# A second MLP whose second products take seven block products for eight in half of its quads, with the order of work found by a list pass of the builder

## The chip, the cores and the metric

The kernel runs on one core of a Trainium2 chip. The time is that of one execution on the device in microseconds, the median of several runs of the same program. One execution was profiled as well; all rows below are of that one.

## The reference

Three stages follow one another, all in float32: an attention without softmax, gated by u, and two MLPs over the same 6016 tokens.

```python
# u, v: (2, 3008, 256); z: (2, 3008, 64); S = 3008
scores = (1.0 / S) * np.matmul(z, z.transpose(0, 2, 1))
x = u * np.matmul(np.maximum(scores, 0.0) ** 2, v)
x = x.reshape(6016, 256)
# first MLP: w_in (256, 2048), w_out (2048, 256), s, b: one number each
r = np.maximum(x @ w_in, 0.0)
x = (s * (r * r) + b) @ w_out
# second MLP: weights of its own of the same shapes
h = x @ w_in2
out = (h * (1.0 / (1.0 + np.exp(-1.702 * h)))) @ w_out2
```

## The kernel before

**Products.** Each float32 operand is split into a high and a low part of the reduced matmul type (fp32r): the high part is a copy by ScalarE (ACT), the low part a subtraction by VectorE (DVE). A block product of 128 by 128 by 512 is then three matmuls of TensorE (PE): low by high, high by low, high by high, all summed in one bank of PSUM. The weights come as float64 and are decoded first by a handful of bit operations (`decode_w`).

**Tiles and stages.** The tokens stand in 12 chunks of 512 (the last two 448), and the MLPs work on pairs of chunks. The hidden 2048 columns are 16 blocks of 128. A *quad* is two hidden blocks by the two chunks of a pair, so a pair has 8 quads. In program order come the attention, the first two chunks of the first MLP (`Mlp`), its other five pairs, and the six pairs of the second MLP: 11 pairs of quads. Layer 0 is the first MLP, layer 1 the second.

**A quad's first product** (`Quad.up`, matmuls in `product`, L672) is a two by two product of blocks and already takes seven block products in place of eight, by sums of weights (s1 to s4, `sum_w`) and of tokens (t1 to t4, `parts_of`); its seven products, 21 matmuls, go into the four banks ps_a to ps_d. ACT saves a bank to SBUF (`save`, L720), DVE adds a saved bank to another one (`join`, L730), ACT applies the activation (L744, L752), and the four values c11, c21, c12, c22 are split into high (L760, ACT) and low (L761, DVE). A bank must have been read before the next product can begin in it.

**A quad's second product** (`Quad.down`, `add_hidden`, L542) takes the four values by the blocks of w_out: eight block products, 24 matmuls, into accumulators accq (two sets of two banks), which sum over the eight quads of a pair. `post` stores the end result: y in layer 0 (L566), the transposed output in layer 1 (L580).

**What sets the order.** The engines each work in the order in which the program issues their instructions. The builder walks over steps (four for a quad), and the second product of a step runs 5 steps behind its first. What lies between is put at a numbered step with a rank in it (`later`, `due`), loads and the splitting of weights at numbers worked out by hand (`when`, `todo`). The split weights of the layer at work are held in SBUF (the 32 tiles of `ring`, the sums in four wide tiles); DMAs of the MLPs are issued by one queue on SyncE (SP).

Of the kernel before, what the change touches and what calls it, by code (L numbers as in the profile page):

```python
# [15 lines left out]
def attention_mlp_mlp_kernel(  # L16
# [24 lines left out]
    nc = tc.nc  # L41
# [16 lines left out]
    WARM = 16  # L58
    NQ = NF // 2
    NP = NM // 2  # L60
    assert DQ == 64 and TAIL == 64 and D == 2 * P and NKT == TPC * NCH
# [4 lines left out]
    mid = ctx.enter_context(tc.tile_pool(name="mid", bufs=1))  # L66
    bits = ctx.enter_context(tc.tile_pool(name="bits", bufs=1))
    ew = ctx.enter_context(tc.tile_pool(name="ew", bufs=2))
# [14 lines left out]
    def mid_tile(name, dtype=F32):  # L83
        kind = name[0]
        return mid.tile([P, CH], dtype, tag="w" if kind == "w" else "zu", name=name, bufs=5 if kind == "w" else 4)
# [24 lines left out]

    u_rows = u.rearrange("b s d -> (b s) d")
# [10 lines left out]
    def load_z(bb, t):  # L122
        n = width(t)
        z0 = begin(bb, t)
        zr = mid_tile(f"zr_{bb}_{t}").rearrange("p (t a) -> p t a", a=32)
# [15 lines left out]
    def split_z(bb, t, part):  # L141
        if part == 0:
            zr = staged.pop(("z", bb, t))
            zt = staged["zt", bb, t] = mid_tile(f"zt_{bb}_{t}")
# [47 lines left out]
    def load_u(m, h):  # L192
        start, n = tokens(m)
        ur = mid_tile(f"ur_{m}_{h}").rearrange("p (t a) -> p t a", a=32)
        for i in range(4):
            nc.sync.dma_start(
                out=ur[32 * i : 32 * i + 32, : n // 32, :],
                in_=u_rows[start : start + n, h * P + 32 * i : h * P + 32 * i + 32].rearrange(
                    "(t b) a -> b t a", b=32
                ),  # L200
            )
        staged["u", m, h] = ur

    def gate(m, h):
        n = tokens(m)[1]
        ur = staged.pop(("u", m, h))
        ut = mid_tile(f"ut_{m}_{h}")
        if m < 2 * LASTC:
            nc.vector.transpose(
                out=ut.rearrange("p (t g a) -> p t g a", t=4, g=4),  # L210
                in_=ur.rearrange("p (g t) a -> p t g a", g=4),
            )
        else:
            nc.vector.transpose(out=ut[:, :n], in_=ur[:, : n // 32, :].rearrange("p t a -> p (t a)"))
        x = xT[m][:, h, :n]
        nc.vector.tensor_tensor(out=x, in0=x, in1=ut[:, :n], op=ALU.mult)


# [3 lines left out]
    def load_w(layer, j, k):  # L222
        w = ((w_in1, w_out1), (w_in2, w_out2))[layer][k].bitcast(U32)
        raw = mid_tile(f"wr_{layer}_{j}_{k}", U32)
        if k == 0:
            src = w[:, j * 2 * P : (j + 1) * 2 * P].rearrange("(k p) f -> p k f", p=P)
            nc.sync.dma_start(out=raw.rearrange("p (k f) -> p k f", k=2), in_=src)
        else:
            nc.sync.dma_start(out=raw, in_=w[j * P : (j + 1) * P, :])
        staged["w", layer, j, k] = raw.rearrange("p (n w) -> p w n", w=2)  # L230

    def decode_w(layer, j, k, part):

        raw = staged["w", layer, j, k]
        low, high = raw[:, 0, :], raw[:, 1, :]
        if part == 0:
            pw = staged["pw", layer, j, k] = bits.tile([P, CH // 2], U32, tag="pw", name="pw")
            nc.vector.tensor_scalar(pw, high, 20, 0x7FF, ALU.logical_shift_right, ALU.bitwise_and)  # L240
        elif part == 1:
            pw = staged["pw", layer, j, k]
            nc.scalar.activation(out=pw, in_=pw, func=AF.Relu, scale=float(2**23), bias=rebias[:, 0:1])
            mt = staged["mt", layer, j, k] = bits.tile([P, CH // 2], U32, tag="mt", name="mt")
            nc.vector.tensor_scalar(mt, high, 0xFFFFF, 0x100000, ALU.bitwise_and, ALU.bitwise_or)
        elif part == 2:
            mt = staged["mt", layer, j, k]
            fr = staged["fr", layer, j, k] = bits.tile([P, CH // 2], F32, tag="fr", name="fr")
            nc.vector.scalar_tensor_tensor(fr, low, 2.0**-32, mt, ALU.mult, ALU.add)
        elif part == 3:  # L250
            pw = staged["pw", layer, j, k]
            nc.vector.scalar_tensor_tensor(pw, high, 0x80000000, pw, ALU.bitwise_and, ALU.bitwise_or)
        else:
            pw, fr = staged["pw", layer, j, k], staged["fr", layer, j, k]
            if k == 0:
                staged["wf", layer, j] = mid_tile(f"wf_{layer}_{j}")
            half = staged["wf", layer, j].rearrange("p (k n) -> p k n", k=2)[:, k, :]
            nc.vector.scalar_tensor_tensor(half, fr, 2.0**-20, pw.bitcast(F32), ALU.mult, ALU.mult)
            if k == 1:
                staged["done", layer, j] = staged.pop(("wf", layer, j))  # L260

    def store_w(layer, j):
        wf[layer, j] = hbm.tile([P, CH], F32, tag=f"wf_{layer}_{j}", name=f"wfh_{layer}_{j}")
        nc.sync.dma_start(out=wf[layer, j], in_=staged.pop(("done", layer, j)))

    def fetch_w(layer, j):
        staged["wf", layer, j] = mid_tile(f"wb_{layer}_{j}")
        nc.sync.dma_start(out=staged["wf", layer, j], in_=wf[layer, j])

    def sum_w(layer, i, part):  # L270

        if part:
# [742 lines left out]
```

## Time and profile before

| | |
|---|---|
| median of 3 runs | 1446.21 us (1444.78 to 1446.44) |
| profiled execution | 1447.46 us, of which its span 1445.7 us |
| TensorE busy | 1432.8 us (99%) |
| ScalarE busy | 1089.7 us (75%) |
| VectorE busy | 1062.3 us (73%) |
| mean of the granted TensorE clock | 0.999 of full speed |

The span runs from the first to the last instruction in the trace; the 1.76 us besides are outside it. A busy time counts an instant once, also where the modelled ends of matmuls overlap. The quads take the time from about 553 us to the end; before that come the attention and the first two chunks of the first MLP.

### The profile page before, as it was taken

Reading aid. Unit: us, or ns where it says so; the run is one execution under the profiler, and the core shown is the slowest. Engines: PE = TensorE matmul, PEld = TensorE weight load, DVE = VectorE, ACT = ScalarE, POOL = GpSimd, SP = SyncE. Lnnn points to the kernel's source line nnn. Section 1 sums busy time; section 2 is a strip of 40 time slices with the busy share of each in tenths; the row PEclk is TensorE's granted clock in tenths of the full one; section 3 lists DMA queues with packets and bytes.
Section 4 is the critical chain, followed back from the end, with each engine's and each line's share of the span. In section 5 each row is a group of like instructions: output and inputs, shape, how many; then the busy total and the mean of one; then the engine's idle time right before and its main releaser. Section 6 shows DMA issues by size and latency. Waiting matters only on the chain.

```text
span 1445.7 us, 19096 instructions
## 1 busy us (share of the span) xinstructions
PE 1432.8 (99%) x6404; PEld 1199.6 (83%) x6404; DVE 1062.3 (73%) x2034; ACT 1089.7 (75%) x2044; POOL 3.0 (0%) x10
## 2 busy tenths in 40 slices
PE   9999999999999999999999999999999999999998
PEld 6888888788888888888888888888888888888897
DVE  7899898798889777878787887885545555555544
ACT  8888787988797787787878778886667566666664
POOL 0000000000000000000000000000000000000000
PEclk9999999999999999999999999999999999999999
DMA  5687984678779625133050413120110202020001
GB/s 124 170 223 197 228 231 99 183 200 205 201 208 211 195 80 151 31 95 81 23 131 23 124 37 110 51 78 0 19 41 1 59 1 59 1 55 1 15 15 26
DMA packets 189731, 143.87 MB, mean 100 GB/s; under 512 B 129920, under 2 KB 153984, under 8 KB 187072
## 3 DMA queue, kind: packets, MB, share of 16 engines
q1 hardware_dynamic: 185840, 141.74, 38.0%
q10 hardware_dynamic: 3664, 0.68, 0.3%
q8 instruction: 50, 0.82, 0.2%
q14 instruction: 49, 0.40, 0.1%
q0 software_dynamic: 128, 0.23, 0.1%
HBM read 87.69 MB, written 54.92 MB: 99 GB/s over the span
## 4 chain that ended last, share of the span: by engine, by line
PE 92%; ACT 3%; DMA 2%; DVE 1%; SPq 0%; issue 0%; ACTq 0%; DVEq 0%
PE accq L542 31%; PE ps_b L672 8%; PE ps_d L672 8%; PE ps_c L672 8%; PE acc L345 4%; PE acc L344 4%; PE acc L349 4%; PE ps_a L672 4%; PE tac L344 4%; PE tac L345 4%; PE tac L349 3%; PE accm L542 3%; PE ps_h L503 3%; PE ps_s L367 2%; PE ps_s L368 2%; DMA R<-H 1%
## 5 line engine op out<-in xcount | busy, mean ns | idle before, releaser
L542 PE MATMUL accq<-hi,w 128*128 128x512 f32 (+1 forms) x1408 | 374.3, 385 | 0.0
L542 PEld LDWEIGHTS accq<-hi,w 128*128 128x128 f32 x1408 | 264.4, 188 | 48.6
L761 DVE TENSOR_TENSOR lo<-a,hi 128x512 fp32r<-128x512 f32 (+1 forms) x352 | 229.9, 674 | 59.9 <-ACT hi L760 59.2
L542 PE MATMUL accq<-lo,w 128*128 128x512 f32 (+1 forms) x704 | 217.5, 385 | 0.0
L760 ACT CAST hi<-a 128x512 fp32r<-128x512 f32 (+1 forms) x352 | 205.3, 607 | 4.6 <-DVE a L754 1.4
L542 PEld LDWEIGHTS accq<-lo,w 128*128 128x128 f32 x704 | 132.2, 188 | 24.4
L720 ACT COPY s<-ps_d 128x512 f32<-128x512 f32 (+1 forms) x88 | 50.8, 577 | 125.4 <-PE ps_d L672 125.4
L744 ACT ACTIVATE a<-a 128x512 f32<-128x512 f32 (+1 forms) x224 | 135.2, 620 | 6.7 <-DVE a L730 6.6
L345 PE MATMUL acc<-hi,v 128*128 128x512 f32 (+1 forms) x336 | 129.0, 384 | 2.0 <-DVE v L190 2.0
L720 ACT COPY s<-ps_b 128x512 f32<-128x512 f32 (+1 forms) x88 | 50.7, 576 | 105.6 <-PE ps_b L672 105.6
L344 PE MATMUL acc<-hi,v 128*128 128x512 f32 (+1 forms) x336 | 128.6, 383 | 0.2 <-ACT v L189 0.2
L730 DVE TENSOR_TENSOR a<-ps_c,s 128x512 f32<-128x512 f32 (+1 forms) x88 | 59.5, 676 | 73.6 <-PE ps_c L672 73.4
L385 DVE TENSOR_TENSOR lo<-a,hi 128x512 fp32r<-128x512 f32 (+1 forms) x166 | 109.3, 658 | 3.7
L374 ACT ACTIVATE a<-a 128x512 f32<-128x512 f32 (+1 forms) x168 | 103.7, 617 | 5.3
L373 ACT ACTIVATE a<-ps_s 128x512 f32<-128x512 f32 (+1 forms) x168 | 96.8, 576 | 9.6 <-PE ps_s L368 9.2
L399 DVE STREAM_TRANSPOSE T<-a 128x512 f32<-128x512 f32 (+1 forms) x120 | 79.7, 664 | 31.5 <-ACT a L374 28.7
L349 PE MATMUL acc<-lo,v 128*128 128x512 f32 (+1 forms) x332 | 100.0, 383 | 0.0
L344 PE MATMUL tac<-hi,v 128*128 128x512 f32 x240 | 94.2, 392 | 2.0 <-DVE x L487 1.6
L345 PE MATMUL tac<-hi,v 128*128 128x512 f32 x240 | 93.7, 390 | 0.0
L730 DVE TENSOR_TENSOR a<-ps_b,s 128x512 f32<-128x512 f32 (+1 forms) x44 | 29.9, 679 | 72.1 <-PE ps_b L672 67.9
L467 DVE TENSOR_TENSOR lo<-R,hi 128x512 fp32r<-128x512 f32 x110 | 74.1, 683 | 6.9 <-ACT hi L464 4.1
L730 DVE TENSOR_TENSOR a<-ps_d,s 128x512 f32<-128x512 f32 (+1 forms) x44 | 29.9, 679 | 66.8 <-PE ps_d L672 49.2
(125 smaller groups left out, 2719.5 us busy)
## 6 DMA issues: line engine op xcount, KB each, us to landing
R<-H SPq DMA_DIRECT2D x100, 256.0 KB, 6.1
H<-T SPq DMA_DIRECT2D x20, 1024.0 KB, 4.8
wb<-wfh SPq DMA_DIRECT2D x52, 256.0 KB, 3.5
wr<-in_moe_w_in_dram SPq DMA_DIRECT2D x32, 256.0 KB, 4.3
wr<-in_moe_w_out_dram SPq DMA_DIRECT2D x32, 256.0 KB, 4.0
wfh<-wf SPq DMA_DIRECT2D x32, 256.0 KB, 2.8
f<-rows SPq DMA_DIRECT2D x16, 512.0 KB, 4.3
H<-T SPq DMA_DIRECT2D x10, 512.0 KB, 2.9
```

What stands on the lines that cost most here:

```text
L344: nc.tensor.matmul(acc[d][:, :n], w[:, 0, cols], hi, start=first, stop=False)
L345: nc.tensor.matmul(acc[d][:, :n], w[:, 1, cols], hi, start=False, stop=last and not whole)
L349: nc.tensor.matmul(acc[d][:, :n], w[:, 0, cols], lo, start=False, stop=last)
L374: nc.scalar.activation(out=a[:, :n], in_=a[:, :n], func=AF.Square)
L385: nc.vector.tensor_tensor(out=lo[:, :n], in0=a[:, :n], in1=hi[:, :n], op=ALU.subtract)
L542: nc.tensor.matmul(acc[d][:, :n], w[:, h, d * P : (d + 1) * P], g[:, :n], start=first and i == 0, stop=last and i == 2,)
L672: nc.tensor.matmul(bank[:, :n], a[h], x[:, g, :n], start=first and j == 0, stop=last and j == 2, skip_group_check=True,)
L720: nc.scalar.copy(out=t[:, : self.n], in_=bank[:, : self.n])
L730: nc.vector.tensor_tensor(out=t[:, :n], in0=bank[:, :n], in1=self.kept[x][:, :n], op=ALU.add)
L744: nc.scalar.activation(out=t[:, :n], in_=v[:, :n], func=f)
L760: nc.scalar.copy(out=hi[:, :n], in_=v[:, :n])
L761: nc.vector.tensor_tensor(out=lo[:, :n], in0=v[:, :n], in1=hi[:, :n], op=ALU.subtract)
```

## The change

**The second products.** In five of the six pairs of the second MLP (all but the last), the quads 1, 3, 5 and 6 also take seven block products for the second product (P1 to P7). Their operands on the tokens' side are c11, c12, c22 and four differences t1 to t4, made by DVE (`less`, L1062), each split into high and low; on the side of the weights a11, a12, a22 and sums s1 to s4. P2, P3 and P4 go into accumulators. P1, P5, P6 and P7 are each summed over the four quads in two banks, ps_a and one of ps_b and ps_d, in a tail behind the last quad of the pair (`tail_of`); ACT saves three states of these banks (`keep`), DVE adds to them (`join`) and adds the sums to the accumulators (`close`).

**The weights of layer 1** are no longer held in SBUF. Through the first MLP's pairs they are decoded, summed, split and stored to HBM (`prepare`), and each pair loads them again: 896 KB for a quad's first product into a wide tile (`load_up`), 128 and 256 KB pieces for the second ones. The ring holds the values g_ of the quads of seven instead. Two pools (9 and 16 tiles) became one of 25 (`cells`).

**The order.** From the end of the first MLP's first two chunks on, all work is recorded as operations with what they read, write and occupy, with a cost for each, and put in order by a list pass: each engine in turn gets the operation that can begin first, among several the one with the earliest due time. What `prepare` does is marked as free and spread over the first 380 us of this pass. For PE the pass may look 16 operations ahead of the program's order. Up to there the order of all engines is as before.

```diff
+    SEVEN = {(1, p): (1, 3, 5, 6) for p in range(NP - 1)}
...
+    def scalar(n, f, reads=(), writes=(), new=(), **more):
+        put("ACT", 0.147 + 0.00072 * n, 0.15, f, reads, writes, new, **more)
+
+    def vector(n, f, reads=(), writes=(), new=(), **more):
+        put("DVE", 0.065 + 0.00105 * n, 0.14, f, reads, writes, new, **more)
+
+    def move(kb, f, reads=(), writes=(), new=(), **more):
+        put("SP", 0.45, 1.6 + kb / 150, f, reads, writes, new, **more)
+
+    def matmuls(count, n, f, reads=(), adds=(), writes=(), new=()):
+        put("PE", count * (n / 2400 + 0.0133), 0.27, f, reads, writes, new, adds)
...
+    def load_up(p, i):
+        kind = "RTTR"[(p * NQ + i) % 4]
+        key = "up", 1, p, i
+
+        def f():
+            t = wide_tile(f"{kind}u_{p}_{i}", F32R)
+            nc.sync.dma_start(out=t[:, : 14 * P].bitcast(F32), in_=up_forms[i])
...
+        move(896, f, [("uf", i, 0), ("uf", i, 1)], [key], [(key, kind)])
...
         def up(self, r):
...
             elif r == 1:
-                self.product(b, s(2), "t2", False, False)
-                self.product(c, s(1), "t1", True, False)
...
+                self.product(c, "s1", "t1", True)
+                self.product(b, "s2", "t2", False)
+                self.save("p5", c)
+                self.save("u2", b)
...
+                if self.seven:
+                    self.split("c11")
+                    self.less("t1", "c21", "c22")
+                    self.less("t3", "c11", "c21")
+                    self.less("t2", "c11", "t1")
+                    self.split("c12")
+                    self.less("t4", "c12", "t2")
+                    for x in ("t4", "c22", "t1", "t2", "t3"):
+                        self.split(x)
+                else:
+                    for x in ("c11", "c22", "c21", "c12"):
+                        self.split(x)
...
+        def less(self, to, x, y):
+
+            def f():
+                if to not in self.place:
+                    self.make(to)
+                nc.vector.tensor_tensor(out=self.get(to), in0=self.get(x), in1=self.get(y), op=ALU.subtract)
...
+        def part(self, i, c, what):
+            n, quad, p = self.n, self.quads[i], self.p
+            if what in ("P2", "P3", "P4"):
+                m, d, form = {"P2": (1, 0, "a12"), "P3": (0, 0, "s4"), "P4": (1, 1, "a22")}[what]
+            else:
+                form = {"P1": "a11", "P5": "s1", "P6": "s2", "P7": "s3"}[what]
...
+                for j, (h, g) in enumerate(quad.terms(c)):
+                    nc.tensor.matmul(
+                        to[:, :n], w[:, h, cols], g[:, :n], start=first and j == 0, stop=False, skip_group_check=True
+                    )
...
+    def tail_of(pair):
+
+        a, b, c, d = pair.some
...
+        return (
+            (part(a, "c22", "P1"), part(b, "c22", "P1"), part(c, "c22", "P1")),
+            (part(d, "c22", "P1"), part(d, "c12", "P2"), part(d, "t4", "P4")),
+            (whole("c11"), part(a, "t1", "P5")),
+            (part(b, "t1", "P5"), part(c, "t1", "P5"), part(d, "t1", "P5")),
+            (whole("c22"), part(a, "t2", "P6")),
+            (part(b, "t2", "P6"), part(c, "t2", "P6"), part(d, "t2", "P6")),
+            (whole("c21"), close(0, 0, "v")),
+            (part(a, "t3", "P7"),),
+            (part(b, "t3", "P7"),),
+            (part(c, "t3", "P7"), part(d, "t3", "P7")),
+            (whole("c12"), close(1, 0, "s1"), close(1, 1, "u3")),
+        )
...
+    REACH, AHEAD, BULK, BULK_BIG, SPREAD = 16, 8.0, 7, 3, 380.0
...
+        extra = [i for i in range(n) if ops[i].free]
+        for x, i in enumerate(extra):
+            latest[i] = SPREAD * x / len(extra)
...
+            for e in pending:
+                among = [i for i in line[:REACH] if not waiting[i]] if e == "PE" else pending[e]
...
+                s0 = min(t for t, _ in picks)
+                s0, i = min(((t, i) for t, i in picks if t <= s0 + 1e-9), key=lambda x: x[1] if e == "PE" else latest[x[1]])
+                if best is None or s0 < best[0]:
+                    best = s0, i, e
```

**PE in the last quad of a pair.** Before, the second products of the second MLP's quads are groups of six rows like these, into the two accumulators of a chunk (w_1_12_1 is block 12 of w_out):

```order
L672 MATMUL ps_d_6339<-op_1_0_2_10215,Rs_3_6382 128x512 x3
L672 MATMUL ps_c_6341<-op_1_0_3_10246,Rs_3_6382 128x512 x3
L542 MATMUL accq0_10628<-hi_11080,w_1_12_1_10512 128x512
L542 MATMUL accq1_10629<-hi_11080,w_1_12_1_10512 128x512
L542 MATMUL accq0_10628<-hi_11080,w_1_12_1_10512 128x512
L542 MATMUL accq1_10629<-hi_11080,w_1_12_1_10512 128x512
L542 MATMUL accq0_10628<-lo_11081,w_1_12_1_10512 128x512
L542 MATMUL accq1_10629<-lo_11081,w_1_12_1_10512 128x512
```

In the changed kernel the same place, the tail of the first pair of the second MLP, has P5 of the quads 1, 3, 5 and 6 (weights d_0_s1), three matmuls each, in the bank ps_a, and then a product of six of quad 7 (d_0_7):

```order
L1155 MATMUL ps_a_6360<-hi_11176,d_0_s1_1_10917 128x512 x2
L1155 MATMUL ps_a_6360<-lo_11187,d_0_s1_1_10917 128x512
L1155 MATMUL ps_a_6360<-hi_11206,d_0_s1_1_10917 128x512 x2
L1155 MATMUL ps_a_6360<-lo_11245,d_0_s1_1_10917 128x512
L1155 MATMUL ps_a_6360<-hi_11217,d_0_s1_5_10943 128x512 x2
L1155 MATMUL ps_a_6360<-lo_11254,d_0_s1_5_10943 128x512
L1155 MATMUL ps_a_6360<-hi_11231,d_0_s1_5_10943 128x512 x2
L1155 MATMUL ps_a_6360<-lo_11261,d_0_s1_5_10943 128x512
L1129 MATMUL accq0_10725<-hi_11252,d_0_7_1_10959 128x512
L1129 MATMUL accq1_10726<-hi_11252,d_0_7_1_10959 128x512
```

A quad of seven so has 3 matmuls for each of seven parts, 21 in place of 24; over the whole order of PE 60 matmuls of 128x512 are fewer.

**PE in the first MLP.** At the start of the first pair of quads, before (accm is an accumulator of the chunks before it; six of its rows stand between the products into the banks, two of them shown):

```order
L672 MATMUL ps_b_6338<-op_0_1_2_6072,Rs_0_5576 128x512 x3
L672 MATMUL ps_c_6341<-op_0_1_3_6111,Rs_0_5576 128x512 x3
...
L542 MATMUL accm0_6049<-lo_6259,w_0_12_1_5344 128x512
L542 MATMUL accm1_6050<-lo_6259,w_0_12_1_5344 128x512
L672 MATMUL ps_b_6338<-op_0_1_4_6139,Rs_0_5576 128x512 x3
```

and in the changed kernel:

```order
L968 MATMUL ps_c_6361<-op_0_1_3_6124,Rs_0_5589 128x512 x3
L968 MATMUL ps_b_6358<-op_0_1_2_6085,Rs_0_5589 128x512 x3
...
L763 MATMUL accm0_6062<-lo_6273,w_12_1_5357 128x512
L763 MATMUL accm1_6063<-lo_6273,w_12_1_5357 128x512
L968 MATMUL ps_b_6358<-op_0_1_4_6152,Rs_0_5589 128x512 x3
```

The two products have changed places, so that between the two into ps_b there are 6 matmuls of other work where there were 9; ps_b must be saved by ACT in between. The changed kernel's order has 95 such places.

**DVE in the first MLP's first pair of quads.** In the changed kernel sums of the second MLP's weights (ws, L353) and their low parts (forms, L462) stand between the sums g_ that read the banks and the low parts of the quad's values:

```order
L1027 TENSOR_TENSOR g_c22_6452<-ps_b_6358,s_p5_6413 128x512
L1078 TENSOR_TENSOR lo_6455<-g_c11_6397,hi_6437 128x512
L1045 SCALAR_TENSOR_TENSOR g_c22_6452<-g_c22_6452 128x512
L353 TENSOR_TENSOR ws_6428<-wf_1_0_6204,ws_6428 128x128
L462 TENSOR_TENSOR forms_0_1_6430<-wf_1_0_6204,forms_0_1_6430 128x256
L462 TENSOR_TENSOR forms_0_2_6450<-wf_1_0_6204,forms_0_2_6450 128x256
L1078 TENSOR_TENSOR lo_6475<-g_c22_6452,hi_6466 128x512
L1027 TENSOR_TENSOR g_c12_6480<-ps_c_6361,s_u2_6422 128x512
L462 TENSOR_TENSOR forms_0_0_6473<-ws_6428,forms_0_0_6473 128x512
```

Before, such sums and low parts stood in the last pair of the first MLP and the first of the second, and the forms of w_out for seven products did not exist.

## Rows read from the trace of the kernel before

**Rows 1.** The page: busy time of each engine over the span.
```profile
span 1445.7 us, 19096 instructions
...
PE 1432.8 (99%) x6404; PEld 1199.6 (83%) x6404; DVE 1062.3 (73%) x2034; ACT 1089.7 (75%) x2044; POOL 3.0 (0%) x10
```

**Rows 2.** Busy time by stretch; columns in the first row.
```profile
core 0: us, PE busy (x) PEld busy (x) DVE busy (x) ACT busy (x) POOL busy (x), PEclk, DMA share, GB/s
100.00:200.00 100.00, 100.00 (x453) 84.75 (x452) 90.22 (x198) 82.78 (x156) 0.00 (x0) 1.00 0.84 212
553.00:635.00 82.00, 82.00 (x363) 67.89 (x363) 66.49 (x130) 63.03 (x117) 0.00 (x0) 1.00 0.28 77
...
880.00:955.00 75.00, 73.90 (x358) 66.56 (x357) 63.60 (x140) 64.50 (x141) 0.00 (x0) 1.00 0.29 88
...
1035.00:1117.00 82.00, 82.00 (x363) 67.95 (x362) 45.69 (x73) 53.13 (x96) 0.00 (x0) 1.00 0.13 26
```

**Rows 3.** PE's waits: us in total, times, longest.
```profile
PE acc L345 <- DVE v L190: 2.0, 4, 0.7
PE tac L344 <- DVE x L487: 1.6, 2, 1.4
...
PE ps_c L672 <- DVE a L730: 1.0, 1, 1.0
```

**Rows 4.** The chain of waits in a quad: start, us, what.
```profile
1345.23 2.72 PE accq L542 x12
1347.95 0.68 PE ps_b L672 x3
...
1355.43 2.72 PE accq L542 x12
```

**Rows 5.** Groups by line and shape: count, busy us, mean ns, idle before.
```profile
L761 DVE TENSOR_TENSOR lo<-a,hi 128x512 fp32r<-128x512 f32 x288 | 191.8, 686 | 48.1 <-ACT hi L760 47.7
...
L566 DVE TENSOR_SCALAR y<-accq,sb,shift 128x512 f32<-128x512 f32 x16 | 12.2, 806 | 4.2 <-PE accq L542 4.2
```

**Rows 6.** Timeline of DVE, 600 to 620 us: start, us, what.
```profile
600.08 0.69 DVE L754 SCALAR_TENSOR_TENSOR a<-a 128x512 f32<-128x512 f32 x1
600.68 0.42 DVE L249 SCALAR_TENSOR_TENSOR fr<-wr,mt 128x256 f32<-128x256 uint32 x1
601.01 0.42 DVE L252 SCALAR_TENSOR_TENSOR pw<-wr,pw 128x256 uint32<-128x256 uint32 x1
...
618.07 0.28 DVE L240 TENSOR_SCALAR pw<-wr 128x256 uint32<-128x256 uint32 x1
618.27 0.29 DVE L245 TENSOR_SCALAR mt<-wr 128x256 uint32<-128x256 uint32 x1
```

**Rows 7.** Timeline of DVE at 557 us, sums of weights.
```profile
557.21 0.28 DVE L282 TENSOR_TENSOR ws<-wb 128x128 f32<-128x128 f32 x1
557.53 0.29 DVE L283 TENSOR_TENSOR ws<-ws,wb 128x128 f32<-128x128 f32 x1
557.74 0.29 DVE L284 TENSOR_TENSOR ws<-wb,wb 128x128 f32<-128x128 f32 x1
557.94 0.28 DVE L285 TENSOR_TENSOR ws<-wb,ws 128x128 f32<-128x128 f32 x1
```

**Rows 8.** Timeline of PE and ACT at a bank's save.
```profile
1013.23 0.84 PE L672 MATMUL ps_a<-op,w 128*128 128x512 f32 x3
...
1013.43 0.59 ACT L720 COPY s<-ps_b 128x512 f32<-128x512 f32 x1 [1.53 <-PE ps_b L672]
```

**Rows 9.** Timeline of ACT, 600 to 606 us.
```profile
601.75 0.59 ACT L720 COPY s<-ps_d 128x512 f32<-128x512 f32 x1 [2.40 <-PE ps_d L672]
602.24 0.63 ACT L760 CAST hi<-a 128x512 fp32r<-128x512 f32 x1
602.76 0.60 ACT L744 ACTIVATE a<-ps_b 128x512 f32<-128x512 f32 x1
```

**Rows 10.** The page: DMA issues, count, KB each, us to landing.
```profile
H<-T SPq DMA_DIRECT2D x20, 1024.0 KB, 4.8
```

More of the change, by code (lines that the diff above doesn't have):

```diff
@@ L232, in decode_w @@
[L232 to L260, printed above, removed]
@@ L547, in add, with end_chunk, post @@
                 stop=last and i == 2,
+                skip_group_check=True,
             )
[L550 to L556 removed]
+    def end_chunk(m, acc, keys):
         for d in range(2):
[L558 to L560 removed]
+            post(0, m, d, lambda d=d: acc[d], [keys[d]])
+    def post(layer, m, h, source, reads):
         start, n = tokens(m)
@@ L639, in parts_of, with f @@
         )[k]
-        nc.vector.tensor_tensor(out=x[to], in0=x[first], in1=x[second], op=ALU.subtract)
+        def f():
+            x = parts(layer, p)
+            if k != 1:
+                x[to] = cell(f"ut{k}_{layer}_{p}")[:, :n]
+            else:
+                x["t3"] = x["b12"]
+            nc.vector.tensor_tensor(out=x[to], in0=x[first], in1=x[second], op=ALU.subtract)
+        keys = [part_key(layer, p, x) for x in (first, second, to)]
+        vector(n, f, keys[:2], [keys[2]], [(keys[2], "cell")] if k != 1 else ())
@@ new lines, in product, with f @@
+        def product(self, bank, form, x, first):
+            n, layer, p, i = self.n, self.layer, self.p, self.i
+            if layer:
+                wkey = "up", 1, p, i
+            elif form[0] == "s":
+                wkey = "room", i // 2
+            else:
+                wkey = "w", 2 * i + (form == "a22"), 0
+            def f():
+                if not banks:
+                    banks.extend(ps.tile([P, CH], F32, tag="ps", name=f"ps_{c}") for c in "bdac")
+                if layer:
+                    a = ups[p, i][form]
+                elif form[0] == "s":
+                    s4 = sums[0, i].rearrange("p h (s f) -> p h s f", s=4)
+                    a = [s4[:, h, int(form[1]) - 1] for h in range(2)]
+                else:
+                    w = wi[0, 2 * i + (form == "a22")]
+                    a = [w[:, h, form != "a11"] for h in range(2)]
+                to = xs[layer, p, x]
+                for j, (h, g) in enumerate(((0, 1), (1, 0), (0, 0))):
+                    nc.tensor.matmul(
+                        banks[bank][:, :n], a[h], to[:, g, :n], start=first and j == 0, stop=False, skip_group_check=True
+                    )
+            key = [("ps", bank)]
+            matmuls(
+                3, n, f, [wkey, ("op", layer, p, x)], *(((), key) if first else (key, ()))
+            )
@@ L782, in attention_mlp_mlp_kernel, with f @@
-    class Turn:
-        def __init__(self, quad, r):
-            self.quad, self.r = quad, r
-            self.late = r == 3
-        def up(self):
-            self.quad.up(self.r)
-        def between(self):
-            pass
-        def down(self):
-            self.quad.down(self.r)
+            def f():
+                self.make(c)
+                nc.vector.tensor_tensor(out=self.get(c), in0=banks[bank][:, :n], in1=self.get(x), op=ALU.add)
+            vector(n, f, [("ps", bank), self.key(x)], [self.key(c)], self.new(c))
@@ new lines, in act, with first, square, both @@
+        def act(self, c, bank=None):
+            n, key = self.n, self.key(c)
+            func = AF.Gelu_apprx_sigmoid if self.layer else AF.Relu
+            def first():
+                if bank is not None:
+                    self.make(c)
+                source = self.get(c) if bank is None else banks[bank][:, :n]
+                nc.scalar.activation(out=self.get(c), in_=source, func=func)
+            def square():
+                nc.scalar.activation(out=self.get(c), in_=self.get(c), func=AF.Square)
+            def both():
+                nc.vector.scalar_tensor_tensor(self.get(c), self.get(c), 0.0, self.get(c), ALU.max, ALU.mult)
+            if self.layer == 0 and c == "c22":
+                vector(n, both, [key], [key])
+                return
+            if bank is None:
+                scalar(n, first, [key], [key])
+            else:
+                scalar(n, first, [("ps", bank)], [key], self.new(c))
+            if self.layer == 0:
+                scalar(n, square, [key], [key])
```

1060 lines of the change are left out of this document (803 added, 257 removed).

## The prediction

> **What bounds the kernel now.** Read the busy times first. TensorE (PE) works 1432.8 us of a span of 1445.7 us, VectorE (DVE) and ScalarE (ACT) about three quarters of it [rows 1]. A share over the whole span hides stages, so the next view is the table by stretch: in the stretches of the attention (100 to 200 us), of the first pair of quads of the first MLP (553 to 635) and of a steady pair of the second MLP (1035 to 1117) PE is busy for every microsecond, at full clock, while DVE goes from 90 to 66 to 46 [rows 2]. The one stretch shown in which PE is short is 880 to 955, by 1.1 us, and the list of PE's waits names it: ps_c behind DVE's sum a. The waits in the attention stay as they are, since the order there is unchanged [rows 3]. Last the chain of waits of a quad: first products in threes, second products in sixes and twelves, and the next quad begins the same pattern 10.20 us later; 12 matmuls take 2.72 us, 0.2267 us each, and 45 of them are the 10.20 [rows 4]. So PE's count of matmuls is the time wherever the other two engines keep up. Two questions decide: how many matmuls go, and whether DVE and ACT still keep up with what they get instead.
>
> **What is removed.** A quad of seven has 21 matmuls in its second product instead of 24. Twenty quads (four in each of five pairs) make 60, and PE's order has just 60 fewer of 128x512. They lie in stretches where PE is never idle, so each is worth its spacing: 60 x 0.2267 = 13.6 us. From both sides: a matmul taken out of a stream without gaps can't give more than its spacing, and gives nothing where something else sets the pace (the terms below).
>
> **What is added in the second MLP.** Per quad of seven DVE gets four differences and three more low parts than before, ACT three more high parts; per pair there are also two sums with a saved bank, four sums with an accumulator, three saves on ACT. Against that, the splitting of weights has left this layer. To price DVE the distance from start to start counts, where it has work waiting: 0.60 us for 512 columns, 0.33 for 256, 0.20 for the simple 256-column form [rows 6] and 0.20 for 128 columns [rows 7]. By DVE's order a middle pair of the second MLP has 105 instructions for 71, 63.0 us of work for 42.6, in a pair of 348 matmuls, 78.9 us: 80%. ACT's order has 110 for 95, at 0.49 to 0.52 us each up to 57 of 78.9 us [rows 9]. Both are lower shares than DVE's 90% of the attention, beside a PE without a gap [rows 2]. I take nothing. In the tails the high and low parts are ordered 10 us of PE work or more ahead of their matmuls, which is the cover; where it is gone, an instruction late costs PE up to its own 0.6 us.
>
> **What is added in the first MLP.** Here nothing is saved: the pairs keep 360 matmuls, 81.6 us. But the second MLP's weights are now decoded, summed and split here (L353 and L462 are new), besides the pair's own work. Counted in DVE's order, the first three of these pairs have 170, 154 and 154 instructions for 129, 124 and 124: the first 88 of 512 columns, 34 of 256, 20 simple and 26 of 128 columns, two of y at 0.72 (its 0.806 less the 0.085 by which neighbours overlap [rows 5, 6]). That is 52.8 + 11.4 + 4.0 + 5.2 + 1.4 = 75 us; the next two give 71.9 and 71.5, and before it was 63.1, 63.3 and 63.0. So DVE goes to 92, 88 and 88% of a pair. Bounds: nothing, as in the attention, where 90% went with a full PE; and 1.1 us a pair as in the nearest row with a loss, where DVE was busy 63.6 of 75, 85% [rows 2, 3]. I take the upper, for all three pairs: 3.3 us. What would be late first is the sum behind a bank (g_c11, g_c12, g_c22) or the low part of a quad's values; behind them wait the next product into that bank and the second product.
>
> **Banks of PSUM.** The builder puts a first product ahead of another where before the order was fixed, so that between the end of one group on a bank and the next product into it there is less other work: in 95 places 6 matmuls, 1.36 us (14 of them with 448 columns, 1.2), where before the least was about 1.8. The chain in between: ACT's copy of ps_b begins 0.20 us after the next group on PE begins, and lasts 0.59 [rows 8], so 0.79 us; by DVE's sum 0.20 + 0.69 = 0.89 [rows 5, 8]. Room remains, 0.47 us or more at 1.36. If each had one full instruction of 0.60 in front, PE would lose 0.89 + 0.60 - 1.36 = 0.13 at each, 12 us in all; nothing if none has. I take nothing: at ACT's and DVE's shares the engine is mid-instruction with some 0.3 us to go, and that fits.
>
> **Transfers.** The second MLP's weights are no longer held in SBUF. Each pair loads them again: 8 of 896 KB and some smaller ones, 15.2 MB with rows, forms and outputs in 78.9 us, 193 GB/s where it was 26. In the attention 212 GB/s went with a full PE [rows 2], 1 MB lands in 4.8 us [rows 10], and SP's order has the big loads 25 us of PE work ahead. Lower end nothing; upper end, all eight late by half their landing, 8 x 2.4 x 5 pairs = 96 us, which nothing in these rows makes likely. I take nothing.
>
> **The sum.** The profiled execution took 1447.46 us, 1.76 outside its span. 1445.7 - 13.6 + 3.3 = 1435.4, with 1.76 it is 1437.2. The runs' median, 1446.21, lies 1.25 below the profiled execution, so I predict 1436 us. The end of the program (last second product, transposes, stores) stands as before.
>
> **Rivals.**
> *DVE pays whole durations.* If DVE's instructions in the crowded pairs followed one another at their durations and not at the shorter distance, 0.69 for 512, 0.42 for 256, 0.29 for the simple ones and for 128 columns [rows 6, 7], the first three pairs would have 89.4, 85.0 and 84.6 us of work in 81.6: 7.8 + 3.4 + 3.0 = 14.2 us lost, against 13.6 gained: 1446.8, no change. For it: an instruction that reads the result of the one before it starts 0.32 after it, not 0.21 [rows 7], and sums of weights are such chains. Against it: neighbours start 0.085 before the one in front ends [rows 6], in stretches as dense as these.
> The Trainium skill, page "VectorE: DVE Perf Modes", section "The DRAIN you can't avoid", states that the next operation does not start until the pipe of the one before is empty, and that one which is not held starts earlier. By its first half the time would be that of this rival; the trace agrees with the second half for neighbours that don't depend on each other.
>
> *Slower: DVE's idle time can't be filled.* In the pairs of the first MLP DVE is idle 15.5 of 82 us [rows 2] beside a full PE. If these are waits on banks and on ACT that stay where they are, the added 11.9 + 8.6 + 8.5 = 29.0 us of DVE work lengthens these pairs by as much: with the 13.6 off the median, 1432.6, that is 1461.6. It decides for slower from the point where under half of the added work (13.6 of 29.0) fits into idle time. For it: one engine in fixed order, in which a sum waiting for a bank holds all behind it. Against it: the attention's 90%.
>
> *Part of the gain goes in bank waits.* The 95 narrow places lose about 0.08 us each, with the 3.3 above some 11 us at most: 1438 to 1443. For it: the narrow places are new, and two of ACT's copies stand next to each other there. Against it: the 0.47 us of room.
>
> *Late weights.* The queue on SP is in order, so that a load which waits for its buffer holds later ones, and PE waits for whole landings; 4.8 us for each of five pairs would be 24 us, 1457. Against it: the 25 us of lead and the attention's 212 GB/s.
>
> **Chances.** The gain with at most 5 us lost, 1431.5 to 1438: 0.56. Part of it kept, 1438 to 1443: 0.18. No change, by DVE's durations or a mixture of waits: 0.11. Slower, by idle time not filled (0.10) or late weights (0.05): 0.15. The three runs of this kernel lie within 0.12%; what is within 0.2%, 2.9 us, counts as the same. Faster 0.74, same 0.11, slower 0.15. The low end, 1431.5, is the whole 13.6 with the 1.1 us of 880 to 955 gone as well; the high end, 1446, takes in most of the case of no change.
>
> **What would show it.** Right: PE's busy time falls by about 13 us, PE stays full in the pairs of both MLPs, a middle pair of the second MLP takes 79 us, DVE is near 75 to 78 us busy in the first pair of the first MLP and ACT about as before. Wrong: PE waits behind g_ sums or lo in 553 to 800 (DVE's load), behind ps_b or ps_c in both MLPs (narrow places), or behind the loads of weights after 955 us. What would make it wrong most easily is DVE's 92%: a share above any stretch of before, in an order that no row of before shows.

## The result, and the profile after

The changed kernel takes 1434.93 us (median of 4 runs, 1433.25 to 1435.43), the kernel before 1446.33 (4 runs): a ratio of 0.9919 with a 95% interval of 0.9901 to 0.9936. It is faster, by 11.4 us.

The page of the changed kernel, its span and busy times, answers to [rows 1]:

```profile
span 1432.9 us, 19432 instructions
...
PE 1420.1 (99%) x6344; PEld 1187.7 (83%) x6344; DVE 1168.6 (82%) x2224; ACT 1116.6 (78%) x2123; POOL 3.0 (0%) x10
```

PE has 60 matmuls fewer and is busy 12.7 us less; DVE has 106 us more to do, and PE's share is still 99%. The stretches show where that goes (columns as in [rows 2]; the last two are steady pairs of the second MLP):

```profile
100.00:200.00 100.00, 100.00 (x454) 84.72 (x453) 91.09 (x201) 83.49 (x158) 0.00 (x0) 1.00 0.83 215
553.00:635.00 82.00, 80.31 (x351) 65.21 (x350) 71.58 (x161) 65.67 (x132) 0.00 (x0) 1.00 0.46 139
635.00:717.00 82.00, 82.00 (x363) 67.93 (x362) 73.89 (x155) 66.83 (x131) 0.00 (x0) 1.00 0.42 122
...
880.00:955.00 75.00, 75.00 (x367) 68.62 (x366) 49.43 (x84) 56.56 (x118) 0.00 (x0) 1.00 0.34 115
...
1034.00:1113.00 79.00, 79.00 (x350) 65.29 (x349) 65.85 (x106) 59.22 (x111) 0.00 (x0) 1.00 0.60 193
1113.00:1192.00 79.00, 79.00 (x350) 65.27 (x349) 65.88 (x106) 59.22 (x111) 0.00 (x0) 1.00 0.60 193
```

A steady pair of the second MLP now fits into 79 us, PE is full in it, DVE went from 46 of 82 to 66 of 79, transfers from 26 to 193 GB/s. In the first MLP PE is short in one stretch only, the first pair, by 1.7 us. In 880 to 955 it is now full.

The chain of waits inside the first pair of the second MLP, in order of time, answers to [rows 4]: a quad of seven puts three matmuls at a time into the accumulators (L1155), where a quad of eight puts six (L1129).

```profile
975.51 0.68 PE accq L1155 x3
...
979.59 0.68 PE accq L1155 x3
...
981.63 0.68 PE accq L1155 x3
982.31 1.36 PE accq L1129 x6
```

The length of each pair, read from PE's timeline as the distance between the first products into ps_a of one pair and of the next (us; the last pair runs to the span's end):

| | start | first MLP, 5 pairs | second MLP, 6 pairs |
|---|---|---|---|
| before | 550.55 | 81.60, 81.60, 81.60, 81.53, 75.39 | 81.36, 81.60, 81.60, 81.60, 81.52, 85.75 |
| changed | 549.18 | 84.44, 81.60, 81.60, 81.53, 73.84 | 81.00, 78.97, 78.97, 78.96, 79.22, 83.59 |

From it the whole difference can be added up. The second MLP gives 12.72 us for 60 matmuls (13.6 by the spacing of [rows 4]); the last pair of the first MLP gives 1.55, the wait of [rows 3] among it; the first pair of quads loses 2.84. Together 11.4, the difference of the medians. The single terms come from one profiled execution of each kernel. The spans differ by 12.8: the other 1.4 lies ahead of the quads, where the order is the same. Quads began at 548 to 549.6 us in the profiles of twelve further kernels with that same order ahead of them; the profiled execution of before was 1.25 us above its median.

The list of PE's waits from 540 to 960 us names the loss of the first pair:

```profile
PE ps_b L968 <- DVE g_c L1027: 0.9, 1, 0.9
PE ps_d L968 <- ACT s_u L1018: 0.7, 1, 0.7
```

And the timeline there shows who was late first (start, us, what, idle before it and its releaser):

```profile
549.35 2.23 SPq L339 DMA_DIRECT2D wb<-wfh  x4
...
551.67 0.38 SPq L275 DMA_DIRECT2D wr<-in_moe_w_in_dram  x1
...
556.70 0.29 DVE L304 TENSOR_SCALAR mt<-wr 128x256 uint32<-128x256 uint32 x1 [3.53 <-DMA wr<-in_moe_w_in_dram]
...
558.39 0.68 DVE L1027 TENSOR_TENSOR g_c<-ps_b,s_p 128x512 f32<-128x512 f32 x1
558.99 0.68 DVE L1078 TENSOR_TENSOR lo<-g_c,hi 128x512 fp32r<-128x512 f32 x1
...
559.12 0.96 PE L968 MATMUL ps_b<-op,w 128*128 128x512 f32 x3 [0.94 <-DVE g_c L1027]
559.59 0.68 DVE L1045 SCALAR_TENSOR_TENSOR g_c<-g_c 128x512 f32<-128x512 f32 x1
...
559.92 0.85 PE L968 MATMUL ps_d<-op,w 128*128 128x512 f32 x3
...
560.30 0.62 ACT L1074 CAST hi<-g_c 128x512 fp32r<-128x512 f32 x1 [1.73 <-DVE g_c L1045]
...
563.54 0.53 PEld L968 LDWEIGHTS ps_d<-op,Rs 128*128 128x128 f32 x3 [0.47 <-ACT s_p L1018]
563.54 0.96 PE L968 MATMUL ps_d<-op,Rs 128*128 128x512 f32 x3
...
564.44 1.13 ACT L1074 CAST hi<-g_c 128x512 fp32r<-128x512 f32 x2
...
565.47 0.58 ACT L1018 COPY s_p<-ps_c 128x512 f32<-128x512 f32 x1
...
565.95 0.59 ACT L1018 COPY s_u<-ps_d 128x512 f32<-128x512 f32 x1
...
566.59 0.96 PE L968 MATMUL ps_d<-op,Rs 128*128 128x512 f32 x3 [0.70 <-ACT s_u L1018]
```

Raw weights are issued at 551.67 behind four loads of 256 KB and land at 556.7. DVE stands for 3.53 us before an instruction of the free work that needs them; behind it in DVE's queue is the sum that reads ps_b, and PE waits for that. ACT, which waits for DVE's values in turn (1.73 us at 560.30), comes to its copy of ps_d at 565.95, 1.4 us after the product into that bank ended (563.54 + 0.96), and PE waits once more. The row of PEld at 563.54 is a weight load that waited for ACT's copy as well; the list of PE's waits does not have it.

### The profile page after: what moved, and what is told of

Same layout as the page of the kernel before. It is cut to its first block, busy times and chain, and to the rows that moved or that the text cites. A ratio compares the mean times of both kernels' runs of the same rounds, so it can differ in the third digit from the quotient of the medians.

```text
span 1432.9 us, 19432 instructions
## 1 busy us (share of the span) xinstructions
PE 1420.1 (99%) x6344; PEld 1187.7 (83%) x6344; DVE 1168.6 (82%) x2224; ACT 1116.6 (78%) x2123; POOL 3.0 (0%) x10
## 4 chain that ended last, share of the span: by engine, by line
PE 89%; ACT 4%; DMA 3%; DVE 2%; SPq 1%; issue 1%; POOL 0%; POOLq 0%; ACTq 0%; DVEq 0%
PE accq L1129 25%; PE ps_d L968 8%; PE ps_c L968 8%; PE ps_b L968 8%; PE ps_a L968 4%; PE acc L558 4%; PE acc L557 4%; PE acc L562 4%; PE tac L557 3%; PE tac L558 3%; PE ps_h L713 3%; PE tac L562 3%; PE accq L1155 3%; PE accm L763 3%; PE ps_s L580 2%; PE ps_s L579 2%
## 5 line engine op out<-in xcount | busy, mean ns | idle before, releaser
L1078 DVE TENSOR_TENSOR lo<-g_c,hi 128x512 fp32r<-128x512 f32 (+1 forms) x392 | 257.0, 673 | 59.0 <-ACT hi L1074 58.8
L1074 ACT CAST hi<-g_c 128x512 fp32r<-128x512 f32 (+1 forms) x392 | 232.2, 615 | 43.0 <-DVE g_c L1045 40.1
L1039 ACT ACTIVATE g_c<-g_c 128x512 f32<-128x512 f32 (+1 forms) x224 | 139.3, 622 | 75.6 <-DVE g_c L1027 75.5
L1129 PE MATMUL accq<-hi,w 128*128 128x512 f32 (+1 forms) x640 | 168.2, 385 | 0.0
L1129 PEld LDWEIGHTS accq<-hi,w 128*128 128x128 f32 x640 | 120.1, 188 | 21.9
L1129 PE MATMUL accq<-hi,d 128*128 128x512 f32 (+1 forms) x448 | 117.2, 382 | 0.0
L597 DVE TENSOR_TENSOR lo<-a,hi 128x512 fp32r<-128x512 f32 (+1 forms) x166 | 109.3, 658 | 3.0
L586 ACT ACTIVATE a<-a 128x512 f32<-128x512 f32 (+1 forms) x168 | 103.7, 617 | 5.5
L1129 PE MATMUL accq<-lo,w 128*128 128x512 f32 (+1 forms) x320 | 97.0, 384 | 0.0
L1129 PEld LDWEIGHTS accq<-hi,d 128*128 128x128 f32 x448 | 84.1, 188 | 14.5
L594 ACT CAST hi<-a 128x512 fp32r<-128x512 f32 (+1 forms) x120 | 72.4, 603 | 3.9
```

What stands on the lines that cost most here:

```text
L586: nc.scalar.activation(out=a[:, :n], in_=a[:, :n], func=AF.Square)
L597: nc.vector.tensor_tensor(out=lo[:, :n], in0=a[:, :n], in1=hi[:, :n], op=ALU.subtract)
L1039: nc.scalar.activation(out=self.get(c), in_=source, func=func)
L1074: nc.scalar.copy(out=t[:, :n], in_=self.get(c))
L1078: nc.vector.tensor_tensor(out=t[:, :n], in0=self.get(c), in1=self.tiles["hi", c][:, :n], op=ALU.subtract)
L1129: nc.tensor.matmul(self.accs[k][:, :n], w[:, h, d * P : (d + 1) * P], g[:, :n], start=k in fresh and j == 0, stop=False, skip_group_check= ...
```

## The experiments

Each kernel is the changed one with the edit shown, compared with the kernel before on the same chip. On these chips the kernel before took 1445.71 to 1446.68 us, so a difference from the changed kernel's 1434.93 is sure to about 1 us; what is smaller is read from the pairs in the traces.

**The order alone.**

```diff
-    SEVEN = {(1, p): (1, 3, 5, 6) for p in range(NP - 1)}
+    SEVEN = {}
```

> Only the order and the reloaded weights of the change are kept; every second product takes eight block products again, so the 60 matmuls are back. If the matmuls are the gain: 13.6 us (60 x 0.2267) above the changed kernel's 1434.9, so 1448.5, and within 2.9 us of the kernel before; PE's waits as in the changed kernel, about 1.6 us at the start of the quads. If the order found by the pass is the gain: 1440 or less.

Measured: 1447.23 us beside 1446.68 of before, ratio 1.0003 (0.9994 to 1.0012). No change: the new order, the one pool and the weights loaded again for each pair give nothing of themselves. That nothing is a sum: the first pair of quads takes 84.11 us, 2.5 more than before, and the last pair of the first MLP 73.84, 1.55 less. The steady pairs of the second MLP take 81.60 us again. DVE's instructions for the seven products go with the edit too (2034 of them, as before the change, in place of 2224):

```profile
PE 1432.5 (99%) x6404; PEld 1199.7 (83%) x6404; DVE 1064.3 (74%) x2034; ACT 1077.9 (75%) x2044; POOL 3.0 (0%) x10
```

The gain is the matmuls'.

**Transfers that the pass takes to land later.**

```diff
-        put("SP", 0.45, 1.6 + kb / 150, f, reads, writes, new, **more)
+        put("SP", 0.45, 3.4 + kb / 150, f, reads, writes, new, **more)
```

> The pass counts on 1.8 us more for each transfer to land (5.6 us for 256 KB in place of 3.8), so that it orders what needs a transfer later. If the loss in the first pair of quads (84.4 us where 81.6 would do) comes from DVE's instruction on raw weights that waited 3.5 us for its transfer, with the sum for ps_b behind it: that wait and the two waits of PE behind it go, 1.6 to 2.8 us less, 1432 to 1433.5. If DVE's load of 92% makes the loss: no change, 1434.9, and the first pair still takes some 84 us.

Measured: 1432.80 us (1432.61 to 1433.11), ratio 0.9906 (0.9891 to 0.9921), inside the forecast, but the first pair takes 83.51 us and not 82. PE's wait for ps_b is gone. DVE still waits for raw weights, shorter, and PE for ps_d. DVE's and then PE's waits in this run:

```profile
DVE pw L295 <- DMA wr<-in_moe_w_in_dram: 2.3, 1, 2.3
```
```profile
PE ps_d L968 <- ACT s_u L1018: 0.7, 1, 0.7
...
PE ps_d L968 <- ACT s_p L1018: 0.2, 1, 0.2
```

So half of the question stayed open: whether ps_d's wait comes from raw weights as well, or from the narrow place. The plan's short landing time alone does not explain the loss: with the longer one 1.9 of the 2.8 us are still there.

**The order of two products.** The products by s2 and s1 and their saves change places, as they stood before.

```diff
-                self.product(c, "s1", "t1", True)
                 self.product(b, "s2", "t2", False)
+                self.product(c, "s1", "t1", True)
-                self.save("p5", c)
                 self.save("u2", b)
+                self.save("p5", c)
```

> The product by s2 is issued ahead of the product by s1 again, as in the kernel before, and the saves in the same order, so that ps_b and ps_d have 9 matmuls of other work in front of the next product in place of 6. If the narrow places cost nothing beside a gap of 1.36 us: within 1 us of 1434.9. If each cost about 0.05 us or more: 2 to 5 us less.

Measured: 1433.82 us (1433.28 to 1434.06), ratio 0.9912 (0.9899 to 0.9926), which overlaps the changed kernel's. The pairs behind the first are as in the changed kernel to 0.2 us (81.60, 81.60, 81.53, 73.84, 81.04, 78.95, 79.00, ...), and the first pair takes 83.90; its second wait is now for s_p in place of s_u. The edit did what the forecast says in the first MLP only: PE's timeline has no product there any more that stands 6 matmuls behind the one before on its bank, while in the second MLP 53 such places are left (51 in the changed kernel). So in the first MLP the wait for ps_d stays with the narrow places gone, and the three pairs of 81.60, 81.60 and 81.53 take as long with eight narrow places each, in the changed kernel, as with none. For the second MLP this run tests nothing.

**The last pair too.**

```diff
-    SEVEN = {(1, p): (1, 3, 5, 6) for p in range(NP - 1)}
+    SEVEN = {(1, p): (1, 3, 5, 6) for p in range(NP)}
```

> The last pair of the second MLP (448 columns) takes seven block products in the same four quads too: 12 matmuls fewer at 0.202 us, 2.4 us. Behind the program's last matmul there now stand a sum and a transpose for each of two halves instead of one transpose: about 1.9 us more at the end. By the count and the end: 1434.4, 0 to 1 us below the changed kernel. If the tail's operands come late with nothing behind to cover them: 3 us or more above it.

Measured: 1433.21 us (1432.62 to 1434.20), ratio 0.9909 (0.9896 to 0.9923), 1.7 below the changed kernel but with overlapping intervals. In the profile the last pair takes 83.39 us in place of 83.59: PE's last matmul ends 2.1 us earlier in it, and 1.9 are given back behind it, as forecast, where sums and transposes follow one another on DVE. Whether it is worth anything can't be told from this run.

**More quads.** The tail was written for any number of quads (the parts P1, P5, P6 and P7 in threes), with more free steps behind it.

```diff
-    NTAIL = 7
+    NTAIL = 10
...
-    SEVEN = {(1, p): (1, 3, 5, 6) for p in range(NP - 1)}
+    SEVEN = {(1, p): (1, 2, 3, 4, 5, 6) for p in range(NP - 1)}
```

> Quads 1 to 6 take seven: 30 matmuls fewer than in the changed kernel, 6.8 us. DVE 71.4 of 77.5 us, 92%, in every steady pair of the second MLP. By the count: 1428. If 92% is more than DVE can keep up with beside the bank waits: 1432 or more.

Measured: 1426.70 us (1425.88 to 1428.16), ratio 0.9870 (0.9854 to 0.9885). 8.2 us less for 30 matmuls, 6.8 by the count; steady pairs of 77.54 to 77.57 us for 342 matmuls, which is 0.2268 each. Against the kernel before on its own chip (1445.71) the step is 7.6. In the two profiles the second MLP gives 7.4 of it, 0.6 more than the count, since its pairs no longer stand above their count, and the first pair of quads 0.5 (83.97 in place of 84.44).

With five quads (1, 2, 3, 5, 6) and 8 free steps:

> Quads 1, 2, 3, 5 and 6 take seven block products in the same five pairs: 15 matmuls fewer again, 3.4 us. DVE's order then has 67 us of work by distances of start in a pair of 78.2 us, 86%. If the count of matmuls goes on setting the time: 1431.5. If the tail, longer by four groups, or DVE runs out of cover: 1434 or more, with PE waiting behind low parts.

Measured: 1432.82 us (1431.78 to 1433.73), ratio 0.9913 (0.9899 to 0.9927), 2.1 below the changed kernel. In this kernel 8 free steps are too few: the last part of P7 (L1155) goes into a bank that the next pair already uses (L968), so it computes other sums:

```profile
1037.31 0.84 PE L968 MATMUL ps_b<-op,Tu 128*128 128x512 f32 x3
...
1039.35 0.63 PE L1155 MATMUL ps_b<-hi,d_s 128*128 128x512 f32 x2
```

The pairs take 78.7 to 79.1 us where 345 matmuls would be 78.2. Its time stands for nothing but itself.

With seven (0 to 6):

> Quads 0 to 6 take seven in the five pairs: 45 matmuls fewer than in the changed kernel, 10.2 us. DVE's order then has 74 to 77 us of work by distances of start in a pair of 339 matmuls, 76.9 us: 96 to 100%. If DVE can be filled to the end, as in the run with more work on DVE in the first MLP: 1424.7. If beside the quads' own chains (differences, high and low parts with an end in time) it can't, since this work is not free to wait: PE waits behind g_ or low parts, and 1428 or more.

Measured: 1425.73 us (1424.71 to 1426.19), ratio 0.9855 (0.9839 to 0.9871): 1.0 below six quads with overlapping intervals (1.9 when each is taken against the kernel before on its own chip), where the count says 3.4. Two of its pairs of the second MLP:

```profile
1105.00:1182.00 77.00, 76.96 (x339) 63.35 (x338) 75.90 (x126) 62.90 (x120) 0.00 (x0) 1.00 0.65 207
...
1259.00:1336.00 77.00, 77.00 (x341) 63.57 (x340) 76.64 (x128) 64.05 (x120) 0.00 (x0) 1.00 0.65 203
```

DVE is at 99% and PE is all but full. The pairs take 76.98 to 77.40 us for 339 matmuls (76.84), so DVE's limit shows but has not yet become the bound.

**More work for DVE in the first MLP.**

```diff
+                for _ in range(4):
-                vector(cols.stop - cols.start, lo, list(reads) + [key], [key], free=True)
+                    vector(cols.stop - cols.start, lo, list(reads) + [key], [key], free=True)
```

> Each low part of the second MLP's weights is subtracted four times in place of once, some 50 us of DVE work more in the first four pairs of the first MLP (81.5, 78.4, 77.5 and 78.5 us by distances of start, in 81.6 each); nothing else is added. If DVE's idle time can be filled to the end: 1435 to 1438. If what counts is durations (about 96, 92, 91 and 93 us): 40 us or more above the changed kernel. If idle time can be filled to about 92% only: 10 to 25 us above.

Measured: 1435.19 us (1434.35 to 1435.72), ratio 0.9926 (0.9912 to 0.9940), 0.3 above the changed kernel. DVE is busy 46 us more (1214.6 against 1168.6), and the four pairs take 84.38, 81.62, 82.06 and 81.85 us, together 0.7 more than in the changed kernel. The stretches:

```profile
635.00:717.00 82.00, 82.00 (x363) 67.80 (x362) 77.52 (x165) 63.68 (x125) 0.00 (x0) 1.00 0.29 84
717.00:798.00 81.00, 80.90 (x357) 66.59 (x357) 78.47 (x164) 67.65 (x132) 0.00 (x0) 1.00 0.32 91
798.00:880.00 82.00, 82.00 (x363) 67.58 (x362) 80.81 (x174) 64.15 (x125) 0.00 (x0) 1.00 0.35 101
```

DVE is busy 80.8 of 82 us, and the pair there (81.85) is 0.3 us longer than with 65.2 of 82. Idle time of DVE could be filled nearly to the end here, at 0.7 us for 46.

**Twice the transfers.**

```diff
+            spare = hbm.tile([P, 14 * P], F32, tag=f"spare_{p}_{i}", name=f"spare_{p}_{i}")
+            nc.sync.dma_start(out=spare, in_=up_forms[i])
             nc.sync.dma_start(out=t[:, : 14 * P].bitcast(F32), in_=up_forms[i])
```

> In front of each 896 KB load of weights a copy of the same 896 KB from HBM to HBM goes through the same queue, some 7.2 MB more read and 7.2 MB more written a pair. If the loads' 25 us of lead covers them: 1435 to 1436, with landings longer. If the transfers of the second MLP were near their limit: PE waits behind loads of weights, 5 us or more.

Measured: 1433.74 us (1433.13 to 1434.01), ratio 0.9916 (0.9902 to 0.9930). A steady pair of this run, and its loads, which landed after 4.6 us in the changed kernel:

```profile
1034.00:1113.00 79.00, 79.00 (x350) 65.28 (x349) 65.89 (x106) 59.21 (x111) 0.00 (x0) 1.00 0.82 286
```
```profile
Ru<-uf SPq DMA_DIRECT2D x24, 896.0 KB, 7.1
Tu<-uf SPq DMA_DIRECT2D x24, 896.0 KB, 6.1
```

At 286 GB/s and with loads landing 1.5 and 2.5 us later PE is full.

**Free work held back at the start.** In the pass, free operations may not begin in its first 14 us.

```diff
             t = ready[i]
+            if op.free:
+                t = max(t, 14.0)
```

> The free work (loads, decoding and splitting of the second MLP's weights) may not begin in the first 14 us of the pass; all else as in the changed kernel. With later landings (the run before on this question) PE's wait for ps_b was gone, but DVE still waited 2.3 us for raw weights and PE 0.9 us for ps_d, and the first pair took 83.5 us. If both waits go back to raw weights that hold DVE's queue, and by it ACT's: no wait of PE at the start of the quads, the first pair at about 81.6 us and 1432.1 (2.8 us below the changed kernel). If ps_d's wait comes from the narrow place itself: 83.0 us or more, with the 0.7 us behind s_u still there.

Measured: 1432.63 us (1431.60 to 1433.48), ratio 0.9901 (0.9887 to 0.9916), 2.3 below the changed kernel. The first pair takes 81.90 us, 2.5 less than in the changed kernel, and the list has no wait of PE left in the quads:

```profile
553.00:635.00 82.00, 82.00 (x362) 67.52 (x362) 73.61 (x159) 65.91 (x130) 0.00 (x0) 1.00 0.42 126
```

Both waits came from the free work of those 14 us. The edit holds back all of it, loads, DVE's and ACT's instructions together, so this run doesn't separate the landing of raw weights from the instructions that stand around it. The run with later landings shows both at work: there the sum for ps_b begins at 556.24, behind the wait for raw weights, and the sum for ps_c at 560.12, with forms of the free work (L462) in front of it besides; for it ACT waits 1.04 us on its way to ps_d. The rows of that run:

```profile
556.24 0.68 DVE L1027 TENSOR_TENSOR g_c<-ps_b,s_p 128x512 f32<-128x512 f32 x1
...
559.52 0.68 DVE L462 TENSOR_TENSOR forms<-ws,forms 128x512 fp32r<-128x512 f32 x1
...
560.12 0.68 DVE L1027 TENSOR_TENSOR g_c<-ps_c,s_u 128x512 f32<-128x512 f32 x1
...
560.84 0.63 ACT L1039 ACTIVATE g_c<-g_c 128x512 f32<-128x512 f32 x1 [1.04 <-DVE g_c L1027]
```

The narrow place of ps_d is where ACT's delay came out, not where it arose: it is as narrow in this run (product into ps_d, six matmuls, product into ps_d) and costs nothing.

**All together.** Six or seven quads, in all six pairs, with the free work held back:

> Quads 1 to 6 take seven in all six pairs of the second MLP, and the free work begins 14 us later. By the counts: 1426.7 of the six quads, less 2.3 for the held free work and some 2 for the last pair (18 matmuls of 448 columns, 3.6 us, less a longer end): 1422. If the parts don't add up, since the last pair's tail with six quads has nothing behind to cover it: 1425 or more.

Measured: 1423.61 us (1423.30 to 1424.15), ratio 0.9841 (0.9828 to 0.9854), between the two forecasts: 1.6 of the parts are missing. In the profiles the last pair gives 1.2 us of the 2 counted on (83.60 against 84.84 with six quads in five pairs).

> The same with quads 0 to 6: 15 matmuls of 512 and 3 of 448 columns fewer than with six quads, 4.0 us by the count, 1418. In the run with seven quads DVE was at 99% of the pairs and they took 0.1 to 0.5 us more than their matmuls, so some 2 us of it should be kept: 1420. If DVE's queue falls behind where free work no longer gives way: at or above the six quads.

Measured: 1422.00 us (1421.24 to 1423.48), ratio 0.9833 (0.9819 to 0.9846), the fastest of all, 24.5 us below the kernel before and 12.9 below the changed one. It is 2.0 above the forecast: seven quads against six are worth 1.6 us of the 4.0 in the count, at 76.9 to 77.5 us a pair. One pair of the first MLP takes 82.16 us in this run, with a wait of 0.3 us for ps_d behind s_u, long after the first 14 us; a narrow place can cost something after all when ACT is late.

## Why the prediction was right, step by step

**What bounds the kernel**: right. PE's count of matmuls is the time in the quads: 60 fewer gave 11.4 us, none fewer gave none (the order alone), 30 fewer again gave 8.2 (7.6 against the kernel before on its own chip).

**What is removed**: 13.6 forecast, 12.7 measured in the second MLP. The 0.9 us can be added up. Each of the three steady pairs saved 2.63, where 12 matmuls are 2.72 (together 0.27 short, in a few groups of three matmuls that take 0.69 or 0.70 us in place of 0.68; why stays open). The pair before the last saved 2.30, 0.42 short, and most of that is one wait for a bank, too short for the list, in these rows of the changed kernel:

```profile
1278.08 0.68 DVE L1225 TENSOR_TENSOR k_u<-accq,k_u 128x512 f32<-128x512 f32 x1
...
1278.67 0.68 DVE L1027 TENSOR_TENSOR g_c<-ps_c,s_u 128x512 f32<-128x512 f32 x1
...
1279.62 0.86 PE L968 MATMUL ps_c<-op,Tu 128*128 128x512 f32 x3
...
1279.92 0.57 ACT L1018 COPY s_p<-ps_d 128x512 f32<-128x512 f32 x1
...
1280.54 0.96 PE L968 MATMUL ps_d<-op,Tu 128*128 128x512 f32 x3
```

The three sums of the tail stand in front of the sum for ps_c here (in the pair before, the last of them stands behind it), ACT's copy of ps_d ends at 1280.49, and PE begins its next group 0.92 us after the one before, in place of 0.68. In the last pair the matmuls end 2.7 us earlier, as counted, but the program runs on for 6.9 us behind PE's last matmul in place of 6.4. The forecast let the end stand as before. In the other profiles of kernels with this end it lasts 6.5 to 8.3 us, so whether the change or chance made it longer can't be told. Against these the first pair of the second MLP gives 0.36 without a matmul fewer. PE's last rows, before and after, with spans of 1445.7 and 1432.9:

```profile
1438.98 0.36 PE L542 MATMUL accq<-lo,w 128*128 128x448 f32 x1
```
```profile
1425.60 0.37 PE L1129 MATMUL accq<-lo,d 128*128 128x448 f32 x1
```

**DVE in the first MLP**: the size was near (3.3 forecast, 2.84 measured), the reason was wrong. I put 1.1 us on each of three pairs for DVE's load. The second and third pairs, with DVE busy 73.9 and 73.3 us, lost nothing, and 80.8 of 82 lost 0.3. All of the loss lies in the first pair and comes with the free work of its first 14 us, a transfer that DVE waits for first of all; the run with held free work took 2.5 us of it away. The sign that was set for DVE's load, PE behind a sum g_ between 553 and 800, did come, and stood for something else; the 75 to 78 us of DVE in the first pair did not come (71.58, and 73.61 with the free work held back). The nearest row that I took the price from, 880 to 955 us, was a wait of PE for one sum and not a measure of DVE's load. The step that failed is the upper bound taken for all three pairs; the part named as first to be late, the sum g_ behind a bank, was the right one.

**The wait of 880 to 955**: I left it out of the sum and had it only in the low end. It went: 1.55 us gained in that pair, with a new order and with DVE at 49.4 of 75 us in place of 63.6; which of the two did it isn't separated.

**The sum**: near by some luck. The removal came out 0.9 us smaller than forecast, the loss of the first pair 0.5 smaller, and the 1.55 of the wait stood in no term; together that is the 1.1 us between 1436 and the measured time.

**Narrow places**: right but for a remainder. The list has no wait in any pair behind the first, and the pairs of the first MLP take the same with narrow places and without. In the second MLP a bank cost 0.3 us once (at 1280.5, above), in the tail, which the term did not look at.

**Transfers**: right for the second MLP's weights, with room to spare (286 GB/s). I looked only there, though: the transfer that DVE stood for was a raw-weight load of 256 KB in the first MLP, at the one point where the pass begins and eight loads of 256 KB are issued within 5 us.

**The rivals.** *DVE pays whole durations*: it would have given 1446.8, and 40 us more with the added low parts; neither came. The Trainium skill, page "VectorE: DVE Perf Modes", section "The DRAIN you can't avoid", is borne out in its second half, that an instruction which is not held starts earlier: in the changed kernel DVE's three instructions from 558.39 us on start 0.60 us apart at 0.68 of duration each. *DVE's idle time can't be filled*: refuted by the same run. *Bank waits*: 0.3 us at one place of the second MLP, where up to 11 were priced; the two waits of the first pair are the free work's. *Late weights*: none in the second MLP; the mechanism, a queue in order and an instruction behind it, appeared in small in the first.

## What to carry to other kernels

When PE is full, count its matmuls and then ask of the other engines only whether they have room; with an order made ahead, DVE could be filled here to 80.8 of 82 us with work that has no end in time, and to 76.6 of 77 with the quads' own, at 0.0 to 0.6 us a pair. Where such an order begins, look at what is in flight already: the loss came from the first 15 us, and keeping background work out of that stretch gave back 2.3 us, where a longer landing time in the plan gave back only part. An engine in fixed order makes each instruction that waits for a transfer a wait of all behind it, so the transfer's price is that of the sum standing behind it (3.53 us of DVE's wait, 0.94 of PE's, at 559.12).

## What the runs showed of the hardware

After a wait PE does not go on at its pace at once: the three matmuls behind the wait for ps_b took 0.80 us to the next group (559.12 to 559.92), where such a group takes 0.68 elsewhere. So waits of 1.6 us in the list stood for 2.84 us of a longer pair; two smaller delays behind weight loads (0.47 and 0.4 us of PEld's waiting, which the list of PE leaves out) took 0.5 of it.
